# Rows scattered by expert and rank, and ten tiles of expert 0 beside the transforms

## The chip, the core and the metric

The kernel runs on one core of one Trainium2 chip. The metric is the device time of one execution in microseconds; before the change it is 1528.51 us, the median of 3 runs (1526.93 to 1528.54). Engines are named as the profile names them: PE (TensorE), DVE (VectorE), ACT (ScalarE), POOL (GpSimd) and SP (SyncE, which here only issues DMAs).

## What is computed

Three layers follow one another on 4 sequences of 3072 rows with 256 features (12288 rows in all): the real part of a Fourier transform along both axes, a mixture of 8 experts that sends each row to one expert, and a channel mix with the row before. Cut to what matters:

```python
X = np.fft.fft(np.fft.fft(x, axis=1), axis=2).real          # 4 x 3072 x 256
logits = (X / |X|) @ (emb / |emb|).T / tau                   # 8 experts
e = argmax(logits); gate = softmax(logits)[e]
y[row] = gate * (relu(X[row] @ w1[e]) @ w2[e])               # w1: 256x1024, w2: 1024x256
xk = mu_k * y + (1 - mu_k) * y_prev                          # y_prev: the row before
xr = mu_r * y + (1 - mu_r) * y_prev
out = sigmoid(xr @ w_r) * (relu(xk @ w_k) ** 2 @ w_v)
```

## The kernel before, in words

**Transform stage** (`transform_phase`). Each sequence is folded on DVE and POOL (`third_steps`, `fold_steps`), multiplied on PE by cosine and sine tables along the sequence (`Group`) and then along the features (`d_products`), which also gives the logits as extra columns. A sequence gives 12 tiles of 2 x 128 rows; four tiles, that is 1024 rows, are a group, and there are 12 groups, three for each sequence. A group's rows stand in one of three buffers `rows`, which POOL opens with a small copy (line 984); ACT copies the products into it.

**Gating** (`gate_group`). For each group DVE finds the largest logit and marks the chosen expert, PE sums the marks, and the result is each row's rank within its expert plus 12288 times the expert: its position (`pi`). The rows themselves are stored densely, in the order of the transform, to `xrows` in DRAM by one SP DMA a group (line 749), 1068 bytes a row: 256 features, two spare words, the row number and 8 shifted logits. Where they belong is kept as a list `perm`: for the first 8 groups POOL scatters row numbers to it, 8 indirect DMAs of 128 words a group, each waiting for the fourth before it:

```python
for i, other in enumerate(done):
    if i != len(done) - 4:
        g.tc.declare_no_dep(ins, other, reason="distinct rows")
```

For the last 4 groups the list is made by comparing on DVE (`one_list`, lines 792 and 793) and multiplying on PE (line 816). SP loads the list twice (line 1015), after groups 6 and 8; PE turns it.

**Expert stage** (`expert_phase`). Each expert has 13 tiles of 128 ranks in four chunks. A chunk's rows are gathered by POOL through the list (`gather_rows`, line 243, one indirect DMA a tile), turned on PE, multiplied by `w1` (tile `ph`, all float32 in two parts and three products, lines 184 to 186), rectified on ACT and DVE (1287, 1288), multiplied by `w2` (`po`), scaled by the gate, and scattered by POOL to `ydram` (lines 176 and 1529). Chunk 0 of expert 0, three tiles, is computed in the transform stage; its rows are gathered through the list of the first 6 groups. From then on the loop does the first layer of a chunk together with the second layer of the chunk before it. Rows past the 13 tiles, or ranks that were not known when a tile was gathered, would be done by a loop `overflow_tiles` with a number of trips read at run time.

**Mix stage** (`mix_phase`). 24 blocks of 512 rows, loaded from `ydram`.

**What sets the order.** Each engine runs its instructions in the order in which they were put out. From the second sequence on a planner (`Plan`) sets this order for the transform stage and the early tiles: it holds tasks with an engine, an assumed cost and a due number (`DUE`), plays them through a simple model of the engines and buffers, and puts each out when the model would start it. The order is fixed when the kernel is built; at run time every engine waits at its own next instruction. DMAs of SP and of POOL each go out in such an order too. The expert stage and the mix are written out by hand.

Of the kernel before, what the change touches and what calls it, by code (L numbers as in the profile page):

```python
# [19 lines left out]
NB = 4  # L20
S = 3072
D = 256
E = 8
# [7 lines left out]
ROW = ID + 1 + E  # L31
# [4 lines left out]
PACK = 574 + 128 + E * CAP  # L36
EARLY = 3
MID = 7
# [3 lines left out]
FIRST_LIST = 6  # L42
SCATTER = 8
DUE = dict(load=-33.18, third=2, fold=-1.16, seq=5.2, copy=2.88, gate=9.92, list=0.73, raw=17.17, split=34.13, lload=4.84,
           lload1=14, midg=6, earlyg=-34.95, early=100, sc=1.0, scm=0.05, schop=6.86, lastl=15.65, gint=4)


BANKS = {"a": 2, "b": 4, "c": 2}
# [12 lines left out]
class Slot:  # L61
    """A buffer of a rotation: the first task that uses it takes it, and it is free when all have."""
# [111 lines left out]
def scatter(g, done, **kw):  # L174
    """Row scatters of one list write distinct rows: each waits only for the fourth before it."""
    ins = g.nc.gpsimd.indirect_dma_start(in_offset=None, oob_is_err=False, **kw).ins  # L176
    for i, other in enumerate(done):
        if i != len(done) - 4:
            g.tc.declare_no_dep(ins, other, reason="distinct rows")
    done.append(ins)  # L180

# [7 lines left out]
def common(g):  # L189
# [7 lines left out]
    g.lastp = ctx.enter_context(tc.tile_pool(name="lastp", bufs=1))  # L197
    g.y = ctx.enter_context(tc.tile_pool(name="y", bufs=6))
# [3 lines left out]
    g.xs = g.inner.enter_context(tc.tile_pool(name="xsp", bufs=3))  # L202
    g.ps = ctx.enter_context(tc.tile_pool(name="ps", bufs=2, space=bass.MemoryType.PSUM))
# [3 lines left out]
    g.epos = pack[:, 192:256]  # L207
    g.ids = pack[:, 256:352].bitcast(I32).rearrange("p (b t s) -> p b t s", b=NB, s=2)
    g.where = pack[:, 352:448].bitcast(I32).rearrange("p (k t) -> p k t", t=8)
    g.tri = pack[:, 448:512].bitcast(BF16)  # L210
    g.smask = pack[:, 512:548].bitcast(BF16)
    g.pat = pack[:, 548:550]
    g.iota = pack[:, 550:563]
    g.segment_expert = pack[:, 563:574]
    g.slot_row = pack[:, 574:702]
    g.tile_row = pack[:, 702:702 + E * CAP]
    g.ones = const.tile([128, 128], BF16, name="ones")
    g.cnt = const.tile([128, E], F32, name="cnt")
    g.cnt_early = const.tile([128, E], F32, name="cnte")
    g.cnt_mid = const.tile([128, E], F32, name="cntm")  # L220
    g.position = const.tile([128, NB, 24], F32, name="position")
    g.late_id = const.tile([128, 24], F32, name="lateid")
# [3 lines left out]
    g.keep = const.tile([128, LAST], F32, name="keep")  # L226
    g.idx = const.tile([128, E * CAP], I32, name="idx")
    g.listed = const.tile([E * CAP, 128], F32, name="listed")
    g.known = const.tile([128, E * CAP], F32, name="known")
    nc.vector.memset(g.ones, 1.0)  # L230
    nc.gpsimd.memset(g.known, 0.0)
    g.half = const.tile([128, 8], F32, name="half")
    nc.vector.memset(g.half, 0.5)
    g.unit = const.tile([128, E + 3], F32, name="unit")
# [3 lines left out]
def gather_rows(g, idx, rows):  # L238
    """Rows of the given indices, one tile for each column."""
    tiles = []  # L240
    for t in range(idx.shape[1]):
        x = g.xg.tile([128, ROW], F32, tag="xg", name="xg")
        g.nc.gpsimd.indirect_dma_start(out=x, out_offset=None, in_=rows,
                                       in_offset=bass.IndirectOffsetOnAxis(ap=idx[:, t:t + 1], axis=0))
        tiles.append(x)
    return tiles


def transform_phase(g):
# [4 lines left out]
    ctx = ExitStack()  # L254
    hat = ctx.enter_context(tc.tile_pool(name="hat", bufs=14))
# [4 lines left out]
    tab = g.big.tile([128, TAB], F32, tag="big", name="tab")  # L260
# [44 lines left out]
    nc.sync.dma_start(out=g.perm, in_=a["perm0"])  # L305
    nc.sync.dma_start(out=g.xrows[0:1], in_=a["dummy"])
# [8 lines left out]
    # the first and second parts have cosines along both axes in A, the third the sines along one  # L315
# [4 lines left out]
    def prepare_rows():  # L320
        """The rows of n = 128, folded."""
# [20 lines left out]
    def prepare_columns():  # L342
        """Column 128, folded."""
# [15 lines left out]
    def turn_rows():  # L359
        """The folded rows of n = 128, each on a partition."""  # L360
# [4 lines left out]
    def prepare_experts():  # L365
        """Scaled expert rows; their transforms are extra columns of the last matrices."""
# [29 lines left out]
    def turn_cols(c):  # L396
        """The folded rows of n = 128 of the first batch, on partition 0."""
# [5 lines left out]
    # folds along all axes, in place  # L403
# [8 lines left out]
    def sum_steps(b, c, v=nc.vector):  # L412
        """The two halves of a chunk, added."""
# [3 lines left out]
    def third_steps(b, p=None, v=nc.vector):  # L417
        """The sum of the thirds, the others' difference, and the first less half the others."""
# [63 lines left out]
    def rows_from_below(b, c):  # L482
        """The folded rows of n = 128, from their partitions to the first."""
# [28 lines left out]
    def column_group():  # L512
        """The transforms of column 128, for the rows of the sine groups that stand for it."""
# [4 lines left out]
        for c, i, m, j, n in ((0, 0, eee, 1, eeo), (1, 0, eee, 1, eeo), (2, 1, oee, 0, oeo)):  # L518
            ps = g.ps.tile([NB, 257], F32, tag="b", bufs=4, name="sq")
# [20 lines left out]
    # groups of the sequence transform: odd frequencies, and two kinds of even ones  # L540
    hats, parts = {}, {}

    class Group:
        COST = {"o": 2, "e": 1, "f": 1}

        def __init__(self, b, c, kind):
# [10 lines left out]
            # the third part has its sines first: these go with the cosines of the second  # L557
# [7 lines left out]
        def step(self):  # L565
            if self.ps is None:
                self.ps = g.ps.tile([128, 512], F32, tag="b", bufs=4, name="sq")
# [6 lines left out]
        def copies(self):  # L574
            """What takes the sums from the banks: (engine, cost, function), independent of each other."""
# [25 lines left out]
        def joins(self):  # L601
            """The frequencies of the other two thirds, from the second and third parts."""
# [21 lines left out]
    def patch(b, k):  # L624
        """Row 0 of the sine groups stands for column 128."""
# [21 lines left out]
    v.memset(run0, 0.0)  # L647
    epos = p1.tile([1, E * 8], BF16, name="epos")
# [21 lines left out]
    def d_copies(n):  # L670
        kt, j = n % 12, n % 4
        rows = groups[n // 4]
        G = rows[:, :, :, ID + 1:ROW]
# [19 lines left out]
    def row_view(b):  # L693
        return g.xrows[1 + b * S:1 + (b + 1) * S].rearrange("(p k) r -> p k r", p=128)
# [1234 lines left out]
```

## Time and profile before

| what | value |
|---|---|
| device time, median of 3 runs | 1528.51 us |
| profiled execution: span, first to last instruction | 1543.1 us |
| profiled execution: own time besides the span | not given by the page |
| PE busy | 1373.3 us, 89% |
| DVE busy | 827.7 us, 54% |
| ACT busy | 748.0 us, 48% |
| POOL busy | 344.6 us, 22% |
| DMA packets | 63277, 103.08 MB |
| mean granted clock of PE | 0.948 |

The span is one execution under the profiler. Busy times are shares of that span; an engine that waits for a semaphore is not busy. A row of a timeline has the start, the duration, the engine, the source line, the operation and its tiles, and in brackets how long the engine had been idle and what ended this.

### The profile page before, as it was taken

The page shows a single profiled execution, that of the slowest core. Times are in us where ns is not written, and L with a number is a line of the kernel's source. Part 1 is how long each engine was busy: PE and PEld are TensorE (multiplying, and loading weights), DVE is VectorE, ACT ScalarE, POOL GpSimd, SP SyncE. Part 2 cuts the span into 40 slices and gives each one's busy share as a digit, 9 for nine tenths or more (in the row PEclk, how much of TensorE's full clock was granted, in tenths as well). Part 3 has the DMA queues.
Part 4 walks back from the last instruction along what each step waited for, and adds up shares of the span by engine and source line. Part 5 has one row for each costly group of instructions (what it writes and reads, how often), then busy time and mean ns, then how long its engine had stood idle before and what let it go on. Part 6 is the DMA issues. An engine that isn't in the chain of part 4 may idle for free. (4 is left out here: it accounts for less than half of the span.)

```text
span 1543.1 us, 23844 instructions
## 1 busy us (share of the span) xinstructions
PE 1373.3 (89%) x9182; PEld 1284.2 (83%) x9182; DVE 827.7 (54%) x1820; ACT 748.0 (48%) x1868; POOL 344.6 (22%) x346
## 2 busy tenths in 40 slices
PE   5872407299999999999999999999999999999999
PEld 4772406199999999999999989999999999999998
DVE  8862206145555555545534256656666666666664
ACT  2441202055454545455545455656565565656563
POOL 5633313434343334343433200000000000000000
PEclk9886758599999999999999999999999999999999
DMA  8955416222232322322211020101010101111000
GB/s 252 220 90 77 43 27 86 85 96 71 71 102 72 101 70 75 98 74 86 72 46 43 32 80 28 55 28 56 28 56 28 56 28 47 37 36 48 15 28 28
DMA packets 63277, 103.08 MB, mean 67 GB/s; under 512 B 8372, under 2 KB 50729, under 8 KB 60970
## 3 DMA queue, kind: packets, MB, share of 16 engines
q1 hardware_dynamic: 46050, 69.84, 17.3%
q0 software_dynamic: 16784, 31.57, 8.0%
q8 instruction: 73, 1.20, 0.4%
q14 instruction: 42, 0.34, 0.1%
q10 hardware_dynamic: 328, 0.12, 0.0%
HBM read 63.17 MB, written 39.77 MB: 67 GB/s over the span
## 5 line engine op out<-in xcount | busy, mean ns | idle before, releaser
L1288 DVE SCALAR_TENSOR_TENSOR hl<-ph,hh 128x384 fp32r<-128x384 f32 (+1 forms) x256 | 150.5, 588 | 237.7 <-ACT hh L1287 236.9
L186 PE MATMUL po<-wh,hl 128*128 128x256 f32 x832 | 235.8, 283 | 20.5 <-DVE hl L1288 20.5
L1287 ACT ACTIVATE hh<-ph 128x384 fp32r<-128x384 f32 (+1 forms) x256 | 132.4, 517 | 249.3 <-PE ph L186 247.9
L1696 DVE SCALAR_TENSOR_TENSOR k<-ph,r 128x512 f32<-128x512 f32 x192 | 132.7, 691 | 224.1 <-ACT r L1694 224.1
L1694 ACT ACTIVATE r<-ph 128x512 f32<-128x512 f32 x192 | 115.0, 599 | 260.3 <-PE ph L186 260.3
L184 PE MATMUL po<-wh,hh 128*128 128x256 f32 x832 | 235.8, 283 | 2.1 <-DVEq L1399 2.1
L185 PE MATMUL po<-wl,hh 128*128 128x256 f32 x832 | 234.2, 281 | 0.0
L184 PE MATMUL po<-wv,hh 128*128 128x256 f32 x768 | 219.5, 286 | 0.7 <-ACT hh L1702 0.7
L185 PE MATMUL po<-wv,hh 128*128 128x256 f32 x768 | 217.0, 283 | 0.0
L186 PE MATMUL po<-wv,hl 128*128 128x256 f32 x768 | 216.6, 282 | 0.4 <-DVE hl L1703 0.4
L176 POOL DMA_INDIRECT ydram<-y,xg x104 | 106.2, 1021 | 315.0 <-ACT y L1529 292.3
L186 PEld LDWEIGHTS po<-wh,hl 128*128 128x128 f32 x832 | 158.4, 190 | 20.7 <-DVE hl L1288 20.7
L184 PE MATMUL ph<-th,wh 128*128 128x384 f32 (+1 forms) x480 | 170.8, 356 | 1.3 <-DVE hl L1288 1.2
L185 PE MATMUL ph<-tl,wh 128*128 128x384 f32 (+1 forms) x480 | 167.6, 349 | 0.0
L186 PE MATMUL ph<-th,wl 128*128 128x384 f32 (+1 forms) x480 | 167.6, 349 | 0.0
L184 PEld LDWEIGHTS po<-wh,hh 128*128 128x128 f32 x832 | 157.8, 190 | 4.9 <-issue 2.5
L185 PEld LDWEIGHTS po<-wl,hh 128*128 128x128 f32 x832 | 158.0, 190 | 2.5
L185 PE MATMUL ph<-mix,wk 128*128 128x512 f32 x384 | 151.8, 395 | 0.0
L186 PE MATMUL ph<-mix,wk 128*128 128x512 f32 x384 | 151.7, 395 | 0.0
L184 PE MATMUL ph<-mix,wk 128*128 128x512 f32 x384 | 151.5, 395 | 0.0
L184 PEld LDWEIGHTS po<-wv,hh 128*128 128x128 f32 x768 | 145.0, 189 | 3.2 <-ACT hh L1702 0.9
L185 PEld LDWEIGHTS po<-wv,hh 128*128 128x128 f32 x768 | 144.4, 188 | 2.1
(264 smaller groups left out, 2849.3 us busy)
## 6 DMA issues: line engine op xcount, KB each, us to landing
wraw<-in_w_dram SPq DMA_DIRECT2D x16, 1024.0 KB
xrows<-rows SPq DMA_DIRECT2D x12, 1068.0 KB
yl<-ydram SPq DMA_DIRECT2D x24, 512.0 KB
out_dram<-ot SPq DMA_DIRECT2D x23, 512.0 KB
xs<-in_xg_dram SPq DMA_DIRECT2D x9, 512.0 KB
xs<-in_xg_dram POOLq DMA_DIRECT2D x9, 512.0 KB
xs<-in_xg_dram SPq DMA_DIRECT2D x3, 1024.0 KB
wide<-in_w_k_dram SPq DMA_DIRECT2D x2, 1024.0 KB
```

Of the source, the lines that this page charges most:

```text
L176: ins = g.nc.gpsimd.indirect_dma_start(in_offset=None, oob_is_err=False, **kw).ins
L184: nc.tensor.matmul(out=out, lhsT=ah, rhs=bh, start=first, stop=False)
L185: nc.tensor.matmul(out=out, lhsT=ah, rhs=bl, start=False, stop=False)
L186: nc.tensor.matmul(out=out, lhsT=al, rhs=bh, start=False, stop=last)
L1287: return (lambda: nc.scalar.activation(out=hh[:, 0:N], in_=ps[:, 0:N], func=ACTF.Relu), lambda: nc.vector.scalar_tensor_tensor(out=hl[:, 0 ...
L1288: lambda: nc.vector.scalar_tensor_tensor(out=hl[:, 0:N], in0=ps[:, 0:N], scalar=0.0, in1=hh[:, 0:N].bitcast(F32), op0=ALU.max, op1=ALU.sub ...
L1694: nc.scalar.activation(out=r, in_=ps, func=ACTF.Relu)
L1696: nc.vector.scalar_tensor_tensor(out=k2, in0=ps, scalar=0.0, in1=r, op0=ALU.max, op1=ALU.mult)
```

## The change

`xrows` becomes 8 regions of 12288 rows, one for each expert, and one dummy row. A group's rows go straight to their place: POOL scatters each of the 8 columns of a group (128 rows, now 1088 bytes each) to `xrows` at `pi`. The dense stores, the list `perm`, its scatters, loads, compares and products are gone. A tile of an expert is 128 consecutive rows, loaded by one SP DMA (`load_rows`). Rows of a tile past the expert's count, or left out, get a row number past the end (`mark_past`, `row_ids`), so that the scatter to `ydram` drops them; for this six copies of the row number widen the row. The last three tiles of each region are filled with dummy rows at the start.

Expert 0's 13 tiles are cut in chunks of 2, 2, 2, 2, 2 and 3 tiles, loaded after 3, 5, 7, 9, 11 and 12 groups; the first five chunks, ten tiles, are planned beside the transforms, with their gates and their scatters to `ydram`, and the sixth is the first chunk of the expert loop. The other experts have chunks of 4, 3, 3 and 3 tiles (3, 4, 3 and 3 before). Buffers change with it: PSUM banks of the transform stage (a 2, b 3 instead of 4, c 2, a new one s 1), two instead of three buffers `xs` in that stage, four instead of six `y`, four new small ones for the early hidden layers.

```diff
+    tails = g.xrows[0:E * NTOK].rearrange("(e n) r -> e n r", e=E)[:, 128 * (CAP - LAST):128 * CAP]
+    nc.sync.dma_start(out=tails, in_=a["dummy"].unsqueeze(0).to_broadcast([E, 128 * LAST, ROW]))
+    nc.sync.dma_start(out=g.xrows[E * NTOK:], in_=a["dummy"])
...
-        stored[n] = plan.task("SP", 0.65, lambda: nc.sync.dma_start(out=row_view(b)[:, kb * 8:kb * 8 + 8],
-                                                                     in_=t["rows"]),
-                              [c[-1], opened[n]], due, [opened[n].uses[0]], 3.1)
...
-        if n < SCATTER:
-            for q in range(8):
-                scattered.append(plan.task("Pool", DUE["sc"], lambda q=q: scatter(
-                    g, g.list_writes, out=g.perm, out_offset=bass.IndirectOffsetOnAxis(ap=t["pi"][:, q:q + 1], axis=0),
-                    in_=g.where[:, n, q:q + 1], bounds_check=E * NTOK - 1), [c[-1]] + scattered[:1], due, [whole],
-                    DUE['scm']))
-            return
...
+        stored[n] = []
+        for q in range(8):
+            stored[n].append(plan.task("Pool", DUE["sc"], lambda q=q: g.group_writes[n].append(scatter(
+                g, g.row_writes, g.row_reads, out=g.xrows,
+                out_offset=bass.IndirectOffsetOnAxis(ap=t["pi"][:, q:q + 1], axis=0), in_=t["rows"][:, q],
+                bounds_check=E * NTOK - 1)), [c[-1]], due, [whole, opened[n].uses[0]], DUE["scm"]))
...
-def gather_rows(g, idx, rows):
+def load_rows(g, e, o, n, later=()):
     tiles = []
-    for t in range(idx.shape[1]):
+    for t in range(o, o + n):
         x = g.xg.tile([128, ROW], F32, tag="xg", name="xg")
-        g.nc.gpsimd.indirect_dma_start(out=x, out_offset=None, in_=rows,
-                                       in_offset=bass.IndirectOffsetOnAxis(ap=idx[:, t:t + 1], axis=0))
+        r = e * NTOK + 128 * t
+        ins = g.nc.sync.dma_start(out=x, in_=g.xrows[r:r + 128]).ins
+        for other in later:
+            g.tc.declare_no_dep(ins, other, reason="rows of later ranks")
+        g.row_reads.append(ins)
         tiles.append(x)
     return tiles
...
+def row_ids(g, e, o, tiles, t, ids):
+    g.nc.vector.tensor_tensor(out=ids[:, t:t + 1], in0=tiles[t][:, ID:ID + 1].bitcast(I32),
+                              in1=g.past[:, e, o + t:o + t + 1], op=ALU.max)
...
+FIRST_CHUNKS = [(0, 2, 3), (2, 2, 5), (4, 2, 7), (6, 2, 9), (8, 2, 11), (10, 3, 12)]
+CHUNKS = [(0, 4), (4, 3), (7, 3), (10, 3)]
...
+    def loads(i, e, first, n, at):
...
+            def fn(t=t):
+                later = [x for j in range(at, 3 * NB) for x in g.group_writes[j]]
+                g.early_tiles[i].extend(load_rows(g, e, t, 1, later))
+
+            out.append(task("SP", 0.65, fn, [x for j in range(at) for x in stored[j]], 4 * at + DUE["rows"], [s], 0.45))
+        return out, places
...
+    for i, chunk in enumerate(FIRST_CHUNKS):
+        early_chunk(i, *chunk)
+    task("DVE", 0.8, mark_rest, [counted[3 * NB], counted[3]], 12 * NB + DUE["mark"])
+    loads(NP + 1, 1, *CHUNKS[0], 3 * NB)
```

`early_chunk` plans, for one chunk, its loads, the turning of its rows on PE, the two layers block by block (`hidden` for 256 rows, then the second layer into bank s), its gates, its row numbers and its scatters.

## Rows read from the trace of the kernel before

**Rows 1.** Stretches: us, busy us (instructions) by engine, PEclk, DMA share, GB/s

```profile
0.00:55.00 55.00, 30.18 (x167) 25.35 (x168) 46.86 (x110) 14.50 (x50) 34.12 (x32) 0.95 0.95 257
55.00:92.00 37.00, 33.34 (x208) 31.07 (x207) 28.91 (x85) 18.07 (x71) 14.14 (x13) 0.85 0.93 179
92.00:120.00 28.00, 20.11 (x129) 18.30 (x126) 19.52 (x59) 11.55 (x42) 12.56 (x10) 0.88 0.42 47
120.00:305.00 185.00, 60.57 (x348) 54.86 (x348) 39.90 (x166) 25.66 (x92) 56.66 (x63) 0.65 0.40 62
305.00:893.00 588.00, 585.19 (x4040) 565.39 (x4039) 282.53 (x708) 302.42 (x889) 224.03 (x227) 1.00 0.24 74
893.00:1543.10 650.10, 643.94 (x4296) 589.23 (x4296) 409.96 (x697) 375.83 (x725) 3.09 (x3) 1.00 0.13 40
```

**Rows 2.** Waits, 55 to 300 us: total us, times, longest us

```profile
POOL perm L176 <- DMA perm<-pack,pi: 102.3, 29, 10.9
...
PE sq L570 <- DMA xs<-colT: 49.1, 4, 20.4
DVE listed L1024 <- DMA listed<-perm: 48.4, 2, 38.3
...
ACT rows L683 <- DMA xrows<-rows: 27.7, 2, 19.2
```

**Rows 3.** Waits of SP, the DMA queue, 20 to 300 us

```profile
SPq L749 <- POOL rows L984: 91.9, 4, 25.8
```

**Rows 4.** Timeline of POOL, 15:92: start, us, instruction [idle before]

```profile
55.35 1.61 POOL L176 DMA_INDIRECT perm<-pack,pi  x1 [1.20 <-DVE pi L768]
```

**Rows 5.** Timeline of POOL, 90 to 345 us

```profile
260.53 0.97 POOL L176 DMA_INDIRECT perm<-pack,pi  x1 [0.30 <-DMA perm<-pack,pi]
261.80 0.97 POOL L176 DMA_INDIRECT perm<-pack,pi  x1 [0.30 <-issue]
...
280.85 0.97 POOL L176 DMA_INDIRECT perm<-pack,pi  x1 [2.24 <-DMA perm<-pack,pi]
...
296.63 1.04 POOL L243 DMA_INDIRECT xg<-xrows,idx  x1 [13.88 <-DVE known L1039]
```

**Rows 6.** Timeline of all engines, 282 to 345 us

```profile
292.88 0.70 SPq L1015 DMA_DIRECT2D listed<-perm  x1
...
295.26 0.23 DVE L1024 CAST listed<-listed 104x128 f32<-104x128 int32 x1 [10.13 <-DMA listed<-perm]
...
303.96 2.41 PE L1101 MATMUL pt<-pack,xg 128*128 128x128 f32 x8 [7.99 <-DMA xg<-xrows,idx]
...
306.20 0.79 PE L184 MATMUL ph<-xT,wh 128*128 128x512 f32 x1
```

**Rows 7.** Timeline of POOL, 340 to 400 us

```profile
341.00 1.04 POOL L176 DMA_INDIRECT ydram<-y,xg  x1 [14.79 <-ACT y L1529]
342.35 0.99 POOL L176 DMA_INDIRECT ydram<-y,xg  x1 [0.30 <-issue]
343.65 0.98 POOL L176 DMA_INDIRECT ydram<-y,xg  x1 [0.30 <-DMA ydram<-y,xg]
344.93 0.98 POOL L176 DMA_INDIRECT ydram<-y,xg  x1 [0.30 <-ACT hh L1287]
```

**Rows 8.** POOL by line, 0 to 305 us: busy us, mean ns, idle before

```profile
L176 POOL DMA_INDIRECT perm<-pack,pi x64 | 69.4, 1085 | 148.6 <-DMA perm<-pack,pi 102.3 <-issue 43.6 <-DVE PR L793 1.3
...
L984 POOL COPY rows<-pack 128x8 int32<-128x8 int32 x12 | 5.9, 888 | 0.0
...
L1317 POOL TENSOR_TENSOR inv<-ss,half 128x3 f32<-128x3 f32 x1 | 0.9, 922 | 0.0
```

**Rows 9.** Stretches of 20 us, columns as in rows 1

```profile
0.00:20.00 20.00, 4.59 (x22) 2.79 (x22) 16.41 (x54) 3.28 (x8) 8.88 (x10) 1.00 0.94 345
20.00:40.00 20.00, 17.46 (x89) 15.02 (x89) 16.04 (x31) 6.45 (x26) 12.32 (x13) 1.00 0.78 166
```

More of the change, by code (lines that the diff above doesn't have):

```diff
@@ L41 @@
 SPECIAL = 2
[L42 to L48, printed above, removed]
+FIRST_CHUNKS = [(0, 2, 3), (2, 2, 5), (4, 2, 7), (6, 2, 9), (8, 2, 11), (10, 3, 12)]
+CHUNKS = [(0, 4), (4, 3), (7, 3), (10, 3)]
+DUE = dict(load=-33.18, third=2, fold=-1.16, seq=5.2, copy=2.88, gate=9.92, raw=17.17, split=34.13,
+           early=100, sc=1.27, scm=0.45, gint=4, mark=10, rows=0)
+NP = len(FIRST_CHUNKS) - 1
+SEGMENTS = E + NP + 1
 class Ctx:
@@ L171, in run, with scatter @@
                     self.ready[n.engine].append(n)
-def scatter(g, done, **kw):
+def scatter(g, done, reads=(), **kw):
     ins = g.nc.gpsimd.indirect_dma_start(in_offset=None, oob_is_err=False, **kw).ins
+    for other in reads:
+        g.tc.declare_no_dep(ins, other, reason="rows that were there before")
     for i, other in enumerate(done):
@@ L796, in gate_group @@
-        lists = [plan.task("DVE", 0.44, lambda q=q: one_list(q), [c[-1]], due + DUE["list"], [own, *place])
-                 for q in range(8)]
-        pending.append((n, place, lists))
-        if kb == 2 or len(pending) == 2:
-            flush_products(plan, b, due + DUE["list"])
-    made, owns, chosen, opened, stored, begun, scattered, pending = {}, {}, {}, {}, {}, [], [], []
-    known = []
-    def flush_products(plan, b, due):
-        lists = list(pending)
-        pending.clear()
-        bank = plan.slot("c")
-        cell = {}
-        def products():
-            acc = cell["acc"] = g.ps.tile([128, E * CAP], F32, tag="c", bufs=2, name="acc")
-            for i, (n, q) in enumerate((n, q) for n, _, _ in lists for q in range(8)):
-                PR = made[n]["PR"]
-                nc.tensor.matmul(out=acc, lhsT=PR[:, q, 0:128], rhs=PR[:, q, 128:128 + E * CAP], start=i == 0,
-                                 stop=i == 8 * len(lists) - 1)
-        def add():
-            part = g.lastp.tile([128, E * CAP], F32, tag="part", name="part")
-            shift_rows(part, cell["acc"], b)
-            tt(out=g.known, in0=g.known, in1=part, op=ALU.add)
-        after = [x for _, _, l in lists for x in l]
-        p = plan.task("PE", 0.045 * 8 * len(lists), products, after, due, [bank] + [x for _, p, _ in lists for x in p])
-        known.append(plan.task("DVE", 0.55, add, [p], due, [bank]))
@@ L1036, in finish_lists @@
-    def finish_lists():
-        end = slice(E * CAP - LAST, E * CAP)
-        tt(out=g.known[:, end], in0=g.known[:, end], in1=g.keep, op=ALU.mult)
-        v.tensor_copy(out=g.idx[:, MID:], in_=g.known[:, MID:])
-    listed = [task("DVE", 0.25, finish_lists, known, 12 * NB + DUE['lastl'])]
-    g.early_tiles = {i: [] for i in range(4)}
-    gathered = {}
-    listed.append(stored[11])
-    early, mid = known_rows
-    early += [stored[i] for i in range(-(-FIRST_LIST // 3) * 3)]
-    mid += [stored[i] for i in range(-(-SCATTER // 3) * 3)]
@@ L1051, in transform_phase @@
-    gdue = {0: DUE["earlyg"], 1: DUE["midg"] + 1, 2: 8, 3: 9}
-    for i, (first, n, after, rows) in enumerate(((0, EARLY, early, -(-FIRST_LIST // 3) * S), (EARLY, MID - EARLY, mid, 3 * S),
-                                                 (MID, 3, listed, 4 * S), (MID + 3, 3, listed, 4 * S))):
-        gathered[i] = [task("Pool", 1.04, lambda i=i, t=t, rows=rows: g.early_tiles[i].extend(
-            gather_rows(g, g.idx[:, t:t + 1], g.xrows[0:1 + rows])), after, 12 * NB + gdue[i], move=0.38)
-            for t in range(first, first + n)]
@@ L1081, in transform_phase @@
+    for i in range(2):
         split[i] = []
@@ L1503, in weigh @@
         gates[i], steps = gate_steps(g, tiles[i], gt_p)
-        weighs.extend(steps)
+        e, o, n = allc[i]
+        ids[i] = gt_p.tile([128, 4], I32, tag="ids", name="ids")
+        weighs.extend([*steps, lambda: [row_ids(g, e, o, tiles[i], t, ids[i]) for t in range(n)]])
     def first_layer(i, fc, tag="a"):
```

468 lines of the change are left out of this document (211 added, 257 removed).

## The prediction

> **What bounds the kernel now.** I read the stretches of the span first, because the shares over the whole run mix two different stages. From 305 us on TensorE (PE) is busy 585.2 of 588.0 us and then 643.9 of 650.1 us at full clock: both the expert stage and the mix are PE alone [rows 1]. Before 305 us it is busy only 144.2 us (the sum of the first four stretches), and from 120 to 305 us just 60.6 of 185 us, at a granted clock of 0.65, that is most of the time at the lower of its two levels [rows 1]. No other engine fills that stretch either: POOL, the next, has 56.7 us. So waits set the transform stage, and the list of waits is read next.
>
> The reader is to see one loop there. POOL waits 102.3 us in 29 pieces for the landing of its own list scatters [rows 2]: each of the 64 scatters of row numbers waits for the fourth before it. The first issues at 55.35 us [rows 4], the last at 280.85 us [rows 5], which is 225.5/63 = 3.58 us for each, while two that wait for nothing stand 1.27 us apart [rows 5]. The small copy that opens the next group's row buffer (L984) stands behind them in POOL's order, so SP's store of the rows waits 91.9 us for it [rows 3], and the copies of `colT` behind that store on SP hold PE for 49.1 us [rows 2]. ScalarE (ACT) waits 27.7 us for those stores [rows 2]. Then comes a tail: VectorE (DVE) waits 48.4 us in two pieces for the loaded list [rows 2]; the second list load goes out at 292.88 us, is used at 295.26 us, the first gather of the next chunk follows at 296.63 us [rows 5], PE turns its rows at 303.96 us and the first product after that is at 306.20 us [rows 6]. I call 306.2 us the hand-over: from there on PE does not stop.
>
> So span = hand-over + remaining expert tiles + mix. After the hand-over 101 of the 104 tiles are left and take 588 us, 5.82 us a tile [rows 1].
>
> **The change, part by part.** *Ten tiles of expert 0 instead of three before the hand-over.* Seven tiles leave the PE-bound stage: 7 x 5.82 = 40.8 us less after the hand-over. They don't vanish; PE has to do them before it. 144.2 + 40.8 = 185 us of PE work then stands before the hand-over [rows 1], and this is a bound on it that I come back to. For the inputs of seed 0, counted from the reference, expert 0 has 351, 573, 829, 1071 and 1304 rows after 3, 5, 7, 9 and 11 groups, where the five chunks need 256, 512, 768, 1024 and 1280, and the largest expert has 1623 of 1664 rows: no overflow tile runs, and that loop costs nothing.
>
> *The lists go.* 64 list scatters, two list loads, 32 pairs of DVE compares with 32 PE products, the 12 dense row stores on SP and the 10 gathers ahead of the hand-over are gone, and with them the waits of rows 2 and 3. What is late next is POOL, because each group's rows now leave through 8 indirect scatters of 128 rows: 96 instead of 64.
>
> *The price of one row scatter.* No row of before shows it. The nearest is the output scatter, 128 rows of 1,024 bytes against 1,088: four in a row start at 341.00, 342.35, 343.65 and 344.93 us, 1.31 us apart, waits for the fourth before included [rows 7]. Below, nothing is cheaper than 1.27 us, the spacing of unblocked list scatters [rows 5]; above, a row scatter that lands as slowly as the list scatters costs 3.58 us. I take 1.31 us, as the output scatter is nearly the same transfer, and add what POOL loses beside busy engines: the mean list scatter took 1.085 us [rows 8] against 0.97 undisturbed, 0.115 x 96 = 11 us.
>
> *POOL's chain.* It starts where the first scatter starts now, 55.35 us, since the work ahead of it is the same. 96 x 1.31 = 125.8 us. Also on POOL from there: 9 openings of row buffers at 0.89 us, 8.0 us; 5 powers for the gates at 0.92 us, 4.6 us [rows 8]; 8 of the 10 early output scatters, 10.5 us: together 23.1 us. 55.35 + 125.8 + 23.1 + 11 = 215.3 us for the last row scatter. Then its landing and the landing of the row load at 2.4 us each (the list load's 292.88 to 295.26) and 2.2 us from the first turning to the first product (303.96 to 306.20) [rows 6], 7.0 us. A third row buffer in flight hides gating and row copies of the next group: a group costs POOL over 10 us, and opening, products, copies and gating of the next two fit beside it. If they don't, the excess is a wait on POOL; I count it under the third rival.
>
> *The fill of the tails.* SP now writes 8 x 384 dummy rows of 1,088 bytes, 3.34 MB, ahead of the loads of batch 2 and ahead of the first row scatter, which waits for it. At the rates of the first two stretches, 345 and 166 GB/s [rows 9], it takes 9.7 to 20 us, starting at about 20 us when the first inputs are in. It can end before 55.35 us at no cost, or push it by up to 15 us; I take 4 us. The Trainium skill (DMA: Bandwidth & Descriptors, Rules for kernel authors) speaks against its form: a DMA whose outermost dimension has fewer than 16 entries, here the 8 experts, is confined to that many of the 16 engines. No row here shows such a DMA. By that rule the fill takes twice as long, 20 to 40 us, and is the fourth rival below.
>
> *Loads on SP in place of gathers.* 104 gathers leave POOL. After 305 us POOL is busy 224 of 588 us beside a full PE [rows 1], so this saves nothing there; nor do 104 more SP loads cost, with a DMA share of 0.24 and two chunks of lead. Without that lead each chunk would wait one landing, 2.4 us, at most 28 x 2.4 = 67 us; I take 0. Before the hand-over each early load waits on SP for eight or more scatters, and behind it in SP's order stand `colT` copies, batch loads and weights. The wait of PE for `colT` is 49.1 us in four pieces now, the longest 20.4 us [rows 2]: between 0 and 49 us, I take 4 us, as SP waits for POOL in both cases but POOL moves 2.7 times faster.
>
> *The rest.* Smaller pools (banks "b" 4 to 3, chunk buffers 3 to 2, y buffers 6 to 4), five markings of late rows, one small DVE operation a tile: DVE is busy 40 of 185 us from 120 to 305 us and half of the expert stage [rows 1], which hides them; uncovered, 94 tiny operations at the 0.2 us of the list's cast would be some 20 us. I take 0.
>
> *The sum.* Hand-over at 215.3 + 7.0 + 4 + 4 = 230 us, 76 us earlier. PE then has 185 us of work in 230; 28.5 us of its idle time already stand before 92 us [rows 1], so from 92 us on it must be 88% busy. It can, but PE is nearly the second bound. Span: 1543.1 - 76.2 - 40.8 = 1426 us. The span of the profiled execution, the only time the page gives of it, is 14.6 us above the median of the runs, 1528.5 us. With PE full after 305 us this difference can hardly lie there; it lies in the stage whose waits shrink. I keep half of it, 7 us: **1419 us**.
>
> **Rivals.** *1, the floor:* scatters at 1.27 us, no loss beside other engines, fill and SP order hidden: hand-over at 55.35 + 121.9 + 23.1 + 7 = 207 us, and the full 14.6 us stay: 1389 us. For it: undisturbed scatters do reach that spacing [rows 5]. Against: DVE, PE and POOL would all be busy at once there, and PE would need to be full.
>
> *2, slower:* the row scatters land like the list scatters, each waiting for the fourth before it, 3.58 us: hand-over at 55.35 + 343.7 + 23.1 + 7 = 429 us, 1618 us. It decides from 2.72 us a scatter on, where the hand-over is 347 us and the 40.8 us are eaten. For it: the wait for the fourth is the same code, and 96 is more than 64. Against: output scatters of nearly the same size keep 1.31 us [rows 7].
>
> *3, order:* early loads and early products stand in fixed orders on SP and PE; where POOL runs late, transform work queued behind them waits, POOL starves and the stage stretches. Priced by about two waits as long as the longest for `colT` now, less the 4 us counted, some 35 us: 1454 us. For it: just this held PE for 49.1 us [rows 2]. Against: the waits that started it were list landings.
>
> *4, the fill holds the inputs:* with a fill of 20 to 40 us from 20 us on, the first scatter and batch 1 come up to some 20 us late, 16 more than counted: 1435 us. For it, DMA is already 0.78 to 0.94 busy in those stretches [rows 9]; against, POOL has some slack before it needs batch 1.
>
> **How the numbers follow.** Forecast 0.50, with its own range 1400 to 1442 us; floor 0.14; order 0.22; fill 0.08; slower 0.06. The predicted time is the forecast's, 1419 us. The range goes from just under the floor to past the order case, 1386 to 1466 us. A difference within 0.2% can't be told from none; only a hand-over at 340 to 352 us would give that, 0.01. Faster 0.93, slower 0.06.
>
> **What would show it.** Right: scatters into `xrows` from about 55 us at 1.3 to 1.5 us; POOL over 80% busy up to about 215 us; the first product of chunk (10, 3) near 230 us; PE full from there with 5.8 us a tile; no wait for lists. Wrong: long idle times of POOL for the landing of its row scatters (second rival), waits of PE for `colT` or of SP for row scatters while POOL idles (third), a first row scatter well after 60 us (fourth), or an expert stage that is no longer full. The prediction falls if the hand-over lies under 200 or over 280 us.

## The result, and the profile after

The changed kernel takes 1472.76 us (median of 4 runs, 1471.09 to 1473.73) against 1528.53 us of the kernel before on the same chip (1526.93 to 1532.35): ratio 0.9622, interval 0.9604 to 0.9641. It is 55.8 us faster; forecast were 109. The later runs were made in five sets, each on one chip and with the kernel before beside it (the expectations say "call"). In three of them TensorE's products came late in the transform stage (pauses, with rows in the last section) and every kernel that ran in both kinds of set, the one before too, took 25 to 46 us longer, so times are only compared within their set.

Stretches of the kernel after (columns as in [rows 1], which they answer; the cuts are the first and last row scatter, the hand-over and the first load of the mix):

```profile
0.00:55.00 55.00, 23.58 (x127) 18.96 (x128) 35.60 (x93) 11.20 (x36) 19.20 (x19) 0.83 0.74 191
55.00:82.00 27.00, 6.51 (x40) 5.95 (x40) 8.27 (x22) 4.67 (x14) 10.21 (x11) 0.63 0.78 145
82.00:205.00 123.00, 93.78 (x639) 84.63 (x639) 69.99 (x218) 61.39 (x205) 89.77 (x88) 0.91 0.45 138
205.00:240.00 35.00, 8.72 (x57) 7.74 (x57) 6.51 (x35) 5.80 (x24) 23.53 (x25) 0.61 0.38 128
240.00:282.50 42.50, 41.61 (x343) 40.33 (x341) 14.98 (x44) 18.43 (x56) 7.48 (x9) 1.00 0.06 20
282.50:824.90 542.40, 539.10 (x3758) 522.45 (x3758) 280.12 (x787) 280.93 (x829) 120.28 (x122) 1.00 0.24 80
824.90:1470.20 645.30, 639.80 (x4296) 584.81 (x4296) 409.70 (x696) 375.92 (x725) 3.06 (x3) 1.00 0.13 41
```

The two last stretches are close to the forecast: 542.4 us for 94 tiles (5.77 us each, PE full) and 645.3 us for the mix, together 8 us less than it had. What went wrong in the mechanism lies before the hand-over, now 282.54 us, in two holes: 55 to 82 us (PE busy 6.5 of 27 us) and 205 to 240 us (8.7 of 35 us). After the second, PE works alone for 42.5 us while POOL has 7.5 us to do.

The first hole, in the timeline of SP (start, duration, engine, line, operation; SPq is SP issuing a DMA):

```profile
13.04 0.82 SPq L331 DMA_DIRECT2D xrows<-in_dummy_dram  x1
13.91 38.41 SPq L332 DMA_DIRECT2D xrows<-in_dummy_dram  x1
52.45 2.96 SPq L533 DMA_DIRECT2D crow<-cev  x2
55.52 6.18 SPq L296 DMA_DIRECT2D xs<-in_xg_dram  x3
```

L331 is the fill of the tails; its 3072 packets run from 18.7 to 68.6 us. The one-row DMA behind it (L332) sits on SP for 38.41 us, so that the loads of batch 2 (L296) go out at 55.52 us. The timeline of POOL has both holes:

```profile
71.03 1.20 POOL L301 DMA_DIRECT2D xs<-in_xg_dram  x1 [40.63 <-DMA xs<-in_xg_dram]
...
81.84 1.11 POOL L178 DMA_INDIRECT xrows<-rows,pi  x1 [0.17 <-issue]
...
228.25 0.97 POOL L178 DMA_INDIRECT xrows<-rows,pi  x1 [0.31 <-issue]
229.53 0.97 POOL L178 DMA_INDIRECT xrows<-rows,pi  x1 [0.30 <-issue]
230.52 2.10 POOL L1288 TENSOR_TENSOR inv<-ss,half 128x2 f32<-128x2 f32 x3
233.71 1.03 POOL L178 DMA_INDIRECT ydram<-y,ids  x1 [1.09 <-ACT y L1134]
```

POOL idles 40.63 us for batch 2, whose additions and folds stand in its order ahead of the scatters: the first row scatter is at 81.84 us, not at 55.35 [rows 4]. From there the scatters run as priced, after one wait of 7.97 us at 95 us, in the end 1.28 us apart without a wait; little is left of the loop of [rows 2], where POOL waited 102.3 us for landings: 14.6 us here. But behind the last, at 229.53 us, stand three gate powers and the first output scatter of the early tiles. PE waits for them:

```profile
210.34 0.19 PE L798 MATMUL pc<-sc,ones 128*128 128x8 bf16 x1
233.84 0.58 PE L1103 MATMUL po<-run,ones 1*128 1x512 bf16 x1 [23.30 <-ACT y L1134]
...
282.54 0.44 PE L195 MATMUL ph<-xT,wfirst 128*128 128x384 f32 x1 [0.93 <-ACT y L1134]
```

ACT can't copy the first chunk's sums (`y`, L1134) before its gate is known; they hold the only bank of tag "s"; L1103 opens the second chunk's sums in that bank, and PE's products put out behind it run after it. So one early chunk, and half of the first layer of the second, is done beside the transforms, and four run alone from 234 to 282 us.

### The profile page after: what moved, and what is told of

Read it like the earlier page. It is cut to its first block, busy times and chain, and to the rows that moved or that the text cites. A ratio compares the mean times of both kernels' runs of the same rounds, so it can differ in the third digit from the quotient of the medians.

```text
span 1470.2 us, 24335 instructions
## 1 busy us (share of the span) xinstructions
PE 1353.1 (92%) x9252; PEld 1264.9 (86%) x9252; DVE 825.2 (56%) x1894; ACT 758.3 (52%) x1888; POOL 273.5 (19%) x275
## 5 line engine op out<-in xcount | busy, mean ns | idle before, releaser
L1259 DVE SCALAR_TENSOR_TENSOR hl<-ph,hh 128x384 fp32r<-128x384 f32 (+1 forms) x232 | 136.6, 589 | 241.0 <-ACT hh L1258 239.8
L1258 ACT ACTIVATE hh<-ph 128x384 fp32r<-128x384 f32 (+1 forms) x232 | 120.0, 518 | 238.6 <-PE ph L197 237.0
L195 PE MATMUL po<-wh,hh 128*128 128x256 f32 x752 | 210.7, 280 | 2.0 <-DVEq L1365 2.0
L197 PE MATMUL po<-wh,hl 128*128 128x256 f32 x752 | 210.3, 280 | 0.0
L196 PE MATMUL po<-wl,hh 128*128 128x256 f32 x752 | 209.8, 279 | 0.0
L178 POOL DMA_INDIRECT ydram<-y,ids x104 | 104.6, 1006 | 439.8 <-DVE ids L265 263.0
L195 PE MATMUL ph<-th,wh 128*128 128x384 f32 (+1 forms) x448 | 158.9, 355 | 0.4 <-DVE hl L1259 0.3
L195 PEld LDWEIGHTS po<-wh,hh 128*128 128x128 f32 x752 | 141.4, 188 | 4.7 <-issue 2.3
L197 PEld LDWEIGHTS po<-wv,hl 128*128 128x128 f32 x768 | 144.5, 188 | 0.6 <-DVE hl L1654 0.6
L196 PEld LDWEIGHTS po<-wl,hh 128*128 128x128 f32 x752 | 141.6, 188 | 2.7
```

Source lines behind the costliest of these rows:

```text
L195: nc.tensor.matmul(out=out, lhsT=ah, rhs=bh, start=first, stop=False)
L196: nc.tensor.matmul(out=out, lhsT=ah, rhs=bl, start=False, stop=False)
L197: nc.tensor.matmul(out=out, lhsT=al, rhs=bh, start=False, stop=last)
L1258: return (lambda: nc.scalar.activation(out=hh[:, 0:N], in_=ps[:, 0:N], func=ACTF.Relu), lambda: nc.vector.scalar_tensor_tensor(out=hl[:, 0 ...
L1259: lambda: nc.vector.scalar_tensor_tensor(out=hl[:, 0:N], in0=ps[:, 0:N], scalar=0.0, in1=hh[:, 0:N].bitcast(F32), op0=ALU.max, op1=ALU.sub ...
```

## Theories

*A/C*: the fill holds the start (A through the 8 entries of its outermost dimension, C through its source, one DRAM row read 3072 times). *B*: the gate powers and output scatters, planned behind all row scatters, hold PE through the bank. Rivals stand with the runs.

## Experiments

**The fill.** *fill16*: in place of the one DMA

```diff
+    for e in range(E):
+        nc.sync.dma_start(out=tails[e], in_=a["dummy"].to_broadcast([128 * LAST, ROW]))
```

> The fill of the tails in the same place of SP's order, as eight transfers of 384 rows, one for each expert, instead of one with 8 entries in its outermost dimension; bytes and packets are the same. Theory A (the form holds half the DMA engines, and SP behind it): the 3072 packets of about 90 ns on 16 engines take some 17 to 25 us instead of 50, SP's next transfers go out by about 35 to 45 us instead of 52, the first row scatter is at 57 to 67 us instead of 81.84, the last at 205 to 215 instead of 229.5, the hand-over some 15 to 25 us earlier than 282.5, the time 1448 to 1460 us instead of 1472.8. Rival A1 (the writes from DRAM to DRAM are limited as such, whatever the form): the fill still ends near 68 us, first row scatter 80 to 84, time 1470 to 1476. Rival A2 (the start doesn't matter, the late tiles of expert 0 set the end): first row scatter early, but time within 3 us of 1472.8.

Ratio 0.9669 (0.9637 to 0.9701), a set with pauses. A1 happened: first row scatter 84.23 us. One stretch of the kernel after, and the same of this one (columns as in rows 1; DMA share and GB/s are the last two):

```profile
20.00:25.00 5.00, 1.82 (x8) 1.04 (x7) 4.93 (x6) 0.00 (x0) 5.00 (x6) 0.73 0.48 89
```

```profile
20.00:25.00 5.00, 3.14 (x12) 2.41 (x11) 4.93 (x5) 0.00 (x0) 5.00 (x6) 1.00 0.89 66
25.00:40.00 15.00, 14.06 (x77) 12.31 (x77) 7.50 (x23) 6.78 (x26) 5.56 (x6) 1.00 0.97 71
```

From 20 to 25 us the engines are busy 0.89 instead of 0.48, and move no more: the median packet takes 190 ns instead of 85. The last ends at 67.6 us (68.6 before this edit). The Trainium skill (DMA: Bandwidth & Descriptors, Rules for kernel authors) names just this form, a leading broadcast of fewer than 16 copies, as confined to at most that many engines. The trace agrees on the engines (a share of 0.48 with 8 copies, 0.89 without); freeing the others bought nothing here. Theory A falls.

*fillrows*: the changed form, but each piece from another place of the input.

```diff
+    flat = a["xg"].rearrange("b c p r d -> (b c p r d)").rearrange("(n f) -> n f", f=2 * D)
+    nc.sync.dma_start(out=tails, in_=flat[0:E * 128 * LAST, 0:ROW].rearrange("(e n) f -> e n f", e=E))
```

> The fill in its form and place as changed (one transfer, 8 entries in its outermost dimension, from DRAM to DRAM, 3072 pieces of 1,088 bytes), but each piece is read from another place of the input, 2,048 bytes apart, instead of all from one row. The contents of the tails play no part in the output, as their row numbers are masked. Theory C (the one source row is the limit, 60 to 64 packets a microsecond): with 7 to 8 packets in flight each takes less than 70 ns instead of 85 to 98, the fill is over by about 45 us instead of 68, SP's next transfers go out by 38 us instead of 52, first row scatter at 56 to 70 us, ratio to the kernel before 0.944 to 0.955. Rival C3 (any such copy from DRAM to DRAM in these small pieces is as slow): packet times, 52 us and 82 us as in the changed kernel, ratio 0.960 to 0.965.

Ratio 0.9534 (0.9507 to 0.9561), a set with pauses, in which an unaltered kernel was not run; in another such set that had 0.9643 (0.9614 to 0.9673). The same 3072 packets, DRAM to DRAM, 8 entries outermost:

```profile
20.00:25.00 5.00, 3.09 (x11) 2.31 (x11) 4.93 (x6) 0.00 (x0) 5.00 (x6) 1.00 0.56 175
```

55 ns a packet there, 175 GB/s instead of 89; the last packet ends at 47.5 us, SP is free at 41.46 us (both a little later than expected) and the first row scatter is at 62.72. So the one row as the source cost some 21 of the fill's 50 us. What sets the other 29 (the 8 entries, the piece size, or DRAM as the source) was not separated: the next run changes all three.

*fillsb*: the same bytes from a tile in on-chip memory, 1024 pieces of 3,264 bytes; *after_b* is the unaltered kernel in the same set, *fillsb_b* a repeat in another.

```diff
+    tail = spare[:, 1, 0:LAST * ROW].rearrange("p (t r) -> p t r", t=LAST)
+    v.memset(tail, 0.0)
+    v.memset(tail[:, :, ID:ID + 1].bitcast(I32), NTOK)
+    for e in range(E):
+        nc.sync.dma_start(out=tails[e].rearrange("(p t) r -> p t r", t=LAST), in_=tail)
...
```

> The fill with the same 3.34 MB at the same place of SP's order, from a tile of 128 x 816 numbers that DVE sets up in the on-chip memory: 1024 pieces of 3,264 bytes in place of 3072 reads of one and the same DRAM row. Eight transfers instead of one made no difference: 14 to 17 packets in flight instead of 7.6, but 190 ns for each instead of 85 to 98. Theory C (the one source row in DRAM limits the fill to 60 to 64 packets a microsecond, whatever the engines): the fill is over by 40 us, SP's loads of batch 2 go out before 40 us, the first row scatter is at 54 to 66 us, the last one 15 to 27 us earlier than in the unaltered kernel of this call; the time 12 to 27 us less. Rival C1 (writing to that buffer is limited to 70 GB/s): the fill ends at 60 to 70 us, first row scatter at 80 to 85 us, no difference. Rival C2 (the first scatter comes early, but the rest of the stage is not led by POOL): first row scatter early, last one less than 8 us earlier, time less than 8 us less.

> The changed kernel once more, unaltered, beside the three others of this call: the yardstick on the chip on which they run. The four runs before it were on a chip on which the kernel before takes 1562 us instead of 1528.5. If that chip delays the transform stage alone, this run takes 1503 to 1512 us there (0.9622 of the kernel before, and the measurement's interval), with single stops of ACT and DVE of 2 to 10 us between 150 and 240 us; on the first chip it would be 1472.8 again.

> The fill from on-chip memory alone, once more, beside the two others of this call. Theory C: 26 us less than the changed kernel on either kind of chip, ratio to the kernel before 0.942 to 0.949. If the pauses of TensorE on the slower kind of chip take the place of the late start: 0.953 to 0.963 there.

fillsb 1448.47 us, ratio 0.944 (0.942 to 0.946); after_b 1474.81, 0.9617 (0.9597 to 0.9638): 26.3 us less. fillsb_b: 0.9467 (0.9443 to 0.9491). SP and POOL of fillsb:

```profile
13.09 7.22 SPq L336 DMA_DIRECT2D xrows<-spare  x8
20.91 0.59 SPq L337 DMA_DIRECT2D xrows<-in_dummy_dram  x1
29.08 1.72 SPq L538 DMA_DIRECT2D crow<-cev  x2
30.91 3.11 SPq L296 DMA_DIRECT2D xs<-in_xg_dram  x3
```

```profile
55.80 2.57 POOL L178 DMA_INDIRECT xrows<-rows,pi  x1 [4.19 <-issue]
...
203.78 0.97 POOL L178 DMA_INDIRECT xrows<-rows,pi  x1 [0.30 <-issue]
```

The last packet of the fill ends at 28.4 us. First scatter 26.0, last 27.1, hand-over 26.3 us earlier than in after_b; the hand-overs of after_b and fillsb:

```profile
284.16 0.44 PE L195 MATMUL ph<-xT,wfirst 128*128 128x384 f32 x1 [0.93 <-ACT y L1134]
```

```profile
257.88 0.44 PE L195 MATMUL ph<-xT,wfirst 128*128 128x384 f32 x1 [0.93 <-ACT y L1138]
```

The late start goes through the whole stage, as C says and C2 denies. after_b was free of pauses.

**Gates and output scatters of the early tiles.** *pow*: in `early_chunk`, due 4 * at + 10 in place of due + 1 (101 and more) for the gate steps and row numbers.

```diff
+        soon = 4 * at + DUE["mark"]
...
-        q = chain([("Pool", 0.46, step(n)), ("DVE", 0.2, step(n + 1))], q, due + 1, **use)
+        q = chain([("Pool", 0.46, step(n)), ("DVE", 0.2, step(n + 1))], q, soon, **use)
...
```

> Only the due times of the early chunks' gate steps are changed (squares, power on POOL, quotient, row numbers): they stand among the row scatters, not behind all of them; the early output scatters stay behind. Theory B (the powers behind the row scatters hold the one bank for the early sums, and with it PE): PE's wait of 23.3 us for the copy of y is gone; with four y buffers two early chunks are done before the last row scatter, a third may wait for the bank; PE busy more than 9 of the 20 us in the stretch in which it was busy 5.4 and 6.2; hand-over 8 to 14 us earlier (one more chunk of 10.4 us done beside), time 1459 to 1466. Rival B1 (PE had no work for lack of landed rows, not of the bank): PE is as idle as before at 200 to 240 us, time 1470 to 1475.

Ratio 0.97 (0.9666 to 0.9735) in a set with pauses and without the unaltered kernel: no gain seen, and nothing settled. PE's wait for `y` is 10.9 us instead of 23.3, but POOL now waits 34.5 us at its powers for ACT, and the last row scatter comes at 288.14 us.

*noroot*: the ten early tiles' gates leave out the square root, one DVE product in its place, so that POOL has no part in them.

> The gates of the ten early tiles leave out the square root: one DVE product with the constant stands in place of POOL's power, so that nothing of these gates stands in POOL's order. Theory B (the powers behind the row scatters hold the one bank of the early sums): PE's wait of over 20 us for the copy of y, and ACT's and DVE's for the power, are gone or much shorter; three of the five early chunks have their first layers done before the last row scatter instead of less than two; hand-over 10 to 21 us earlier than in the unaltered kernel of this call (one or two chunks of 10.4 us), time less by as much. Rival B2 (the output scatters that stay behind give the same wait one chunk later): one chunk gained, 5 to 11 us. Rival B1 (rows land too late for it): under 4 us.

1457.78 us, 0.9502 (0.9481 to 0.9523), 17.0 us less than after_b; hand-over 15.8 us earlier:

```profile
268.38 0.44 PE L195 MATMUL ph<-xT,wfirst 128*128 128x384 f32 x1 [0.93 <-ACT y L1134]
```

The stretch from 205 to 240 us, of after_b and of this kernel:

```profile
205.00:240.00 35.00, 10.22 (x54) 9.23 (x53) 6.35 (x34) 6.77 (x27) 24.75 (x27) 0.56 0.39 131
```

```profile
205.00:240.00 35.00, 27.69 (x226) 26.05 (x225) 13.76 (x56) 13.20 (x40) 24.70 (x26) 0.97 0.31 108
```

Its waits of PE keep one for the third chunk, whose `y` finds the four buffers full until the first output scatter at 239.01 us:

```profile
PE po L1103 <- ACT y L1134: 10.9, 1, 10.9
```

So B holds, by more than the one chunk that B2 allows; the output scatters that B2 names hold PE for the 10.9 us that are left.

*powy*: as pow, and the output scatters due at `soon` too; repeated as *powy_b* and, beside the unaltered kernel (*after_c*), as *powy_c*.

```diff
-                 due + 1, [place, gates], 0.45)
+                 soon, [place, gates], 0.45)
```

> As the run with early gates, and the early output scatters are also due among the row scatters. Theory B: four of the five early chunks are done before the last row scatter; that one comes about 8 to 11 us later than 229.5 (8 output scatters of 1.28 us more ahead of it), the hand-over is at 250 to 265 us instead of 282.5, the time 1440 to 1455 us. Rival B2 (output scatters in POOL's order wait for PE and hold the row scatters behind them): POOL idles for y, last row scatter after 245 us, hand-over no earlier than 272, time 1462 to 1480. Rival B1 (rows land too late for any of it): hand-over unchanged, time 1470 to 1475.

> Early gates and early output scatters among the row scatters with the fill as changed, once more, as the first run was on a chip that delays the transform stage of each kernel. Theory B, with its size from the two runs on the other chip (the run with both edits less the run with the fill alone, 25.5 us): first row scatter at 82 us, four of five early chunks done before the last row scatter, hand-over at 256 to 264 us, ratio to the kernel before 0.942 to 0.949. Rival B2 (the gain came only with the early fill): ratio 0.955 to 0.965.

> The changed kernel unaltered, as the yardstick beside the three others of this call. Where the kernel before takes 1530 us: 1471 to 1476. On a chip on which it takes 1558 to 1562 us and TensorE reports finished work up to 9 us late between 130 and 290 us: 1500 to 1512 us, last row scatter at 255 to 268 us.

> Early gates and early output scatters, the fill as changed, now beside the unaltered changed kernel on the same chip. Theory B: without the pauses of TensorE seen on two chips, hand-over 20 to 28 us earlier than in the unaltered kernel, time 18 to 28 us less; with these pauses, 8 to 20 us less. Rival B2 (only the early fill lets the early output scatters gain): less than 5 us.

All three in sets with pauses: 0.9617 (0.9583 to 0.965), 0.9589 (0.9572 to 0.9606), 0.9592 (0.9562 to 0.9621). powy_b lies in the bracket of its rival, not of B. powy_c takes 7.5 us less than after_c (0.9643, 0.9614 to 0.9673), just short of B's bracket for such a set. In powy_c four chunks are copied before the last row scatter, as B has it, but that comes at 298.9 us instead of 261.4: with PE late, the early scatters hold the row scatters behind them (POOL waits 34.4 us for `y`). That is what B2 of the first run describes. What these edits gain with the fill as changed and without pauses was not run.

**Four tiles instead of ten.** *four*, repeated as *four_b* and *four_c*:

```diff
-FIRST_CHUNKS = [(0, 2, 3), (2, 2, 5), (4, 2, 7), (6, 2, 9), (8, 2, 11), (10, 3, 12)]
+FIRST_CHUNKS = [(0, 2, 3), (2, 2, 5), (4, 3, 12), (7, 3, 12), (10, 3, 12)]
-NP = len(FIRST_CHUNKS) - 1
+NP = 2
...
```

> The changed kernel with four tiles of expert 0 beside the transforms (two chunks of two) instead of ten; its other nine tiles go as three chunks of three into the later stage. Theory B (most of the ten tiles were never done beside the transforms: four of five chunks ran alone after 240 us): the hand-over, now the first product of the third chunk, is at 244 to 252 us, six tiles more at 5.77 us follow it, time 1466 to 1478 us, that is no difference. Rival B3 (the ten tiles do lie beside the transforms, and the late hand-over has another cause that four tiles have too): hand-over at 270 to 283, time 1495 to 1508 us.

> Four tiles of expert 0 beside the transforms instead of ten, once more for the same reason. Theory B: the six further tiles are not beside the transforms in the changed kernel but run alone between 240 and 284 us, so no difference: hand-over (the first product of the third chunk) at 243 to 253 us, ratio 0.957 to 0.967 against 0.962 of the changed kernel. Rival B3 (they are beside the transforms): hand-over near 282 us, ratio 0.98 to 0.99.

> Four tiles of expert 0 beside the transforms instead of ten, beside the unaltered changed kernel on the same chip. Theory B (the six further tiles run alone after the last row scatter in the changed kernel): hand-over (now the first product of the third chunk) 30 to 40 us earlier, time within 5 us of the unaltered kernel. Rival B3 (they lie beside the transforms): hand-over less than 8 us earlier, time 27 to 35 us more (six tiles of 5.77 us).

0.9663 (0.9631 to 0.9695), 0.9659 (0.9643 to 0.9675), 0.9657 (0.9625 to 0.9689). Beside after_c: 1509.22 against 1507.52 us. The hand-overs of after_c and four_c:

```profile
315.80 0.44 PE L195 MATMUL ph<-xT,wfirst 128*128 128x384 f32 x1 [0.93 <-ACT y L1134]
```

```profile
277.23 0.44 PE L195 MATMUL ph<-xT,wfirst 128*128 128x384 f32 x1 [0.93 <-ACT y L1135]
```

The hand-over is 38.6 us earlier, and the stage with six more tiles behind it takes 38.5 us more. (The hand-overs expected of the first two missed by about 30 us, in sets with pauses.) In the changed kernel the six further tiles are worth nothing; this was measured in sets with pauses only.

**Both causes removed.** *sb_powy* is fillsb and powy together, *sb_powy_four* the same with four tiles, *_b* their repeats in one set.

> The fill from on-chip memory together with the early gates and early output scatters among the row scatters. If theories B and C both hold and their terms add: first row scatter at 54 to 66 us, four of five early chunks done before the last row scatter, hand-over 30 to 45 us earlier than in the unaltered kernel of this call, time 0.935 to 0.945 of the kernel before. If C holds and B2 of the run with early output scatters (these wait for PE and hold the row scatters behind them), the last row scatter is later than in the run with the fill alone and the time 0.946 to 0.958 of the kernel before.

> Four tiles instead of ten in the version with both causes removed (fill from on-chip memory, early gates and output scatters). If theory B is right, the further tiles do lie beside the transforms there, and taking six of them away costs 6 x 5.77 = 35 us less what PE gains before the hand-over, 2 to 12 us: 23 to 33 us more than the version with ten, that is a ratio to the kernel before of 0.942 to 0.950 against 0.9276. If the tiles are worth nothing there either (PE is the bound of that stage as well): 0.925 to 0.932.

> Fill from on-chip memory, early gates and early output scatters, once more. On a chip without pauses of TensorE 0.9276 again, last row scatter at 223 us, hand-over at 234 us. On the other kind the output scatters wait for late products in POOL's order, as in the run with them alone (last row scatter 299 us instead of 261, 7.5 us less in all): last row scatter at 245 to 275 us, ratio 0.936 to 0.948.

> The same with four tiles instead of ten, beside it on one chip. Theory B: with both causes removed the six further tiles lie beside the transforms and taking them away costs 15 to 33 us against the run with ten, 0.010 to 0.021 in the ratio. Rival (they are worth nothing there either): less than 6 us.

sb_powy 1422.96 us, 0.9276 (0.9256 to 0.9296), more than the two theories had added up to; again 1422.35, 0.9288 (0.9264 to 0.9312). Against fillsb and fillsb_b of the same sets 25.5 and 27.0 us less. Its stretches to the hand-over, and POOL:

```profile
0.00:56.00 56.00, 30.18 (x168) 24.89 (x169) 48.83 (x112) 15.77 (x50) 31.25 (x29) 0.94 0.96 272
56.00:200.00 144.00, 119.96 (x813) 108.87 (x812) 80.70 (x264) 73.53 (x249) 106.98 (x103) 0.89 0.40 123
200.00:234.50 34.50, 29.56 (x222) 27.27 (x220) 11.27 (x39) 11.85 (x37) 18.49 (x20) 0.95 0.35 111
```

```profile
56.28 2.58 POOL L178 DMA_INDIRECT xrows<-rows,pi  x1 [4.18 <-issue]
...
163.09 0.97 POOL L178 DMA_INDIRECT ydram<-y,ids  x1 [3.11 <-ACT y L1139]
...
223.41 0.98 POOL L178 DMA_INDIRECT xrows<-rows,pi  x1 [0.30 <-issue]
```

Four early chunks are copied (162.3 to 214.2 us) before the last row scatter; the hand-over is 234.48 us:

```profile
234.48 0.45 PE L195 MATMUL ph<-xT,wfirst 128*128 128x384 f32 x1 [1.57 <-DVE xT L1059]
```

sb_powy_four gave 0.9583 (0.9554 to 0.9613), outside both of its brackets; that was in a set with pauses and without the version with ten tiles, which says nothing of the tiles; beside sb_powy_b it takes 1451.79 us, 0.9482 (0.9458 to 0.9507): 29.4 us more. Once both causes are gone, the further tiles lie beside the transforms.

## Why the prediction was wrong

- **The hand-over**, forecast at 230 us, was 282.54: three terms, 26.5 us later start, 12.3 us shorter chain, 38 us longer tail. Behind it the kernel took 1187.7 us where 1196.1 were forecast, which hides 8.4 us.
- **"It starts where the first scatter starts now, 55.35 us, since the work ahead of it is the same"** and the 4 us for the fill are the first step that failed: 26.5 us, of which 4 were counted. The fill was sized by the rates of *other* transfers [rows 9] (10 to 20 us; it took some 50), and the loads behind it on its queue had no term of their own. The fourth rival had the place right and the mechanism wrong: the number of engines alone bought nothing (fill16), the source did (fillrows, fillsb); it priced 20 us in all, the runs 26.3.
- **"Also on POOL from there: ... 5 powers, 8 output scatters"** is the second. The cost was right and the place wrong: they stood behind the row scatters, not among them. POOL's chain is so 147.7 us (81.84 to 229.53) where 160 were forecast, 15.1 of them for these; in sb_powy, where they do stand among them, 167.1. The nine openings of row buffers took 3.6 us where 8.0 were counted. The 15 us after the last row scatter (7, and 8 for fill and SP's order) became 53.0, most of it four chunks at 10 to 14 us. Their due numbers of 100 and more, against at most 54 for row scatters, stand in the code: a planner's numbers are to be read for each engine on which the moved work has a step.
- **The third rival** (order, 1454 us) names the right kind of cause, fixed orders, but not this one: in it POOL starves and transform work waits. Here POOL runs on to the last row scatter, and PE's early products wait for it, through a bank and not through SP's `colT`. A late start as in the fourth rival and a loss by order came together, 26.3 us and 25.5 to 27.0 us, where the sum had 4 and 4.
- **The price of one row scatter** was right: 1.28 us in the steady part, forecast 1.31 plus 0.115. The second rival, 3.58 us as for lists [rows 5], is refuted.
- **PE's floor**: 185 us of work in 230 could be done. sb_powy does 179.7 us of it before its hand-over at 234.48 us. That its 1422.96 us lie so near to 1419 is partly luck: the hand-over is 4.5 us later than forecast, what lies behind it 8.9 us shorter, and the offset (next point) 8.3 us off.
- **Tiles**: 5.77 for 5.82 us. **The half offset** was a mistake: 9.6 us of the error of 53.8 are this. In every execution on record the span is 1.7 to 1.9 us *below* the time of the same execution. So the profiled execution of the kernel before, with a span of 1543.1 us, took about 1545 us (an estimate from this), more than any other of that kernel outside the sets with pauses (1526 to 1537.5 us), and its rows show a long execution. A forecast span of 1426 us meant 1428 us, not 1419. Of the 16 us 4 to 5 lie in the mix (650.1 against 645.3 us); where the others lie stays open.
- **Edits costed at nothing** (smaller pools, marking, SP loads for gathers): PE has no wait of more than 2 us after the hand-over, which bears this out there. The single "s" bank and the four `y` buffers were among them, and were what the late powers worked through.

Open: pow alone and powy with the changed fill were never run in a set without pauses, so how the 25.5 to 27.0 us split between powers and output scatters is known only through noroot (17.0 us with the late start).

## What to carry to other kernels

When a change moves work that has a small step on another, in-order engine, find where that step will stand in that engine's order before counting the work as hidden; five powers of 0.7 us and ten output scatters, put behind 96 row scatters, cost over 25 us. Size a new DMA by its own source, and give what stands behind it in the issuing queue a term. Test parts of a large change by putting one cause right at a time: here two edits of a few lines nearly doubled the gain (110.6 instead of 58.8 us in one set). Compare the span of a profiled execution with the times of the runs before a sum is built on its rows: here it was a long one.

## What the runs showed of the hardware

- 1,088-byte packets that all read one DRAM row, between 20 and 25 us: 89 GB/s at a DMA share of 0.48 with 85 ns a packet, 66 GB/s at 0.89 with 190 ns; the whole fill lasts some 50 us either way. From 3072 different places 175 GB/s (55 ns), 29 us in all. From on-chip memory in pieces of 3,264 bytes the same fill moves 403 GB/s, 10 us in all.
- A DMA issued behind that fill held the issuing queue for 38.41 us, 27.46 us with spread sources.
- Scatters of 128 rows of 1,088 bytes issue every 1.28 us in the steady part. The scatters of 128 single numbers, with the same wait for the fourth before, came 3.58 us apart on average, and two that did not wait 1.27 us apart [rows 5].
- In three of five sets engines that waited for TensorE went on late: in four_b at six places between 150 and 244 us, 1.3 to 5.5 us after the modelled end of the last recorded product, 18 us together; no such place is in the traces of before, after and the two sets without pauses. ACT's row behind the first one (timeline of four_b; "remote" is a wait whose end no recorded instruction explains):

```profile
155.99 0.18 ACT L710 ACTIVATE rows<-db 128x16 f32<-128x16 f32 x1 [7.41 <-remote]
```

Its page has as many matmul records (9198) as that of sb_powy_four_b, which was undisturbed, so missing records don't explain it. What causes it stays open; one chip had it in one set and not in another.
